# Sigmoids one by one behind later passes, weight passes behind them, and more filler matmuls between the first weight parts, in an mLSTM + two-MoE kernel

## The chip, the cores and the metric

One core of one Trainium2 chip runs the whole program in one launch. The metric is the time of an execution on the device in microseconds (us), lower is better. In the profile the engines are PE (matrix multiplies; PEld is its loading of the stationary operand), DVE (vector), ACT (scalar, activation functions), POOL (GpSimd) and SP, which issues the DMAs.

## What is computed

The reference is an mLSTM recurrence over 768 steps (2 batches, 8 heads of width 40), then two feed-forward layers over the 1536 tokens, each 320 to 2048 to 320 with an activation between.

```python
for t in range(S):                                   # per batch and head
    m_new = np.maximum(f_gate[t] + m, i_gate[t])
    f_stab, i_stab = np.exp(f_gate[t] + m - m_new), np.exp(i_gate[t] - m_new); m = m_new
    C = f_stab * C + i_stab * outer(v[t], k[t]);  n = f_stab * n + i_stab * k[t]
    o = 1.0 / (1.0 + np.exp(-o_gate[t]))
    y[t] = o * (C @ q[t]) / np.maximum(np.abs(n @ q[t]), 1.0)
h = x @ w_in;  x = (h - np.tanh(h)) @ w_out          # first layer
h = x @ w_in2; out = (h * np.tanh(softplus(h))) @ w_out2   # second layer
```

## The kernel before

**Tiles and stages.** The recurrence is computed in chunks of 128 steps (6 chunks, 2 batches: 12 jobs, `attention(j)`, lines 296 to 409), two jobs to a block of 256 tokens. A block's result, multiplied by the sigmoid of the o gates, is transposed (`transpose_x`, tile `xT`) and goes into the first layer. That layer runs in tiles of 256 tokens by two weight parts of 128 hidden columns, 16 parts in all: `mm1(i)` fills the PSUM tile `h` with 8 matmuls a part, `tile1(i)` makes the activation `g` of it and splits it into a rounded half `gh` (ACT) and a rest `gl` (POOL), and `mm2(i)` adds 12 matmuls a tile into `acc`, two tiles behind. Block 0 meets only the parts f = 0 to 7 first (tiles 0 to 3, `CUT[0] = 8`), while the weights still arrive.

**Weights.** They come as 64-bit floats and are turned into two rounded 32-bit halves in `conv_w` (lines 185 to 215). For each part f there are a shift on DVE (L196), a scaling pass on ACT (L204, `scaled`), a shift-and-or on DVE (L208, `third`), a rounding copy on ACT (L211, tile `w`, first half) and a subtraction on DVE (L213 and L214, second half). The first four matmuls of a part in `mm1` need L211, the next two L213 and the last two L214 as well.

**What sets the order.** Each engine runs its own instructions in one fixed order. A scheduler writes this order out when the program is built; `with after(x)` makes an instruction stand behind `x` on the same engine, and it adds no wait on the chip. So an instruction that has to wait holds everything behind it on its engine.

**Sigmoids.** `session(c0, c1, ...)` (line 681) issues one sigmoid over 128 x 640 for each chunk and, at its end, a small Exp that loads the other function table again. The sigmoid of chunk 0 runs near the start. Those of chunks 1 to 5 are given out in the loop over tiles, at i = 1, 2 and 3 (line 841), each with one instruction to stand behind. The first of them needs one table load, the Exp behind the last another.

**Fills.** `spin(n)` (line 633) issues n matmuls of 512 columns on constant data; nobody reads them. `keep(3, y)` in `mm1` (line 542) puts three of them behind each of the first six weight parts.

**Attention in between.** `ahead(n)` (line 770) moves the next attention jobs along by steps, so their matmuls (`nb`, `sc`, `it`, `pv`, `st`) stand among those of the tiles. `rest_t` (line 491) makes the decays `uT` and `dec`, once.

Of the kernel before, what the change touches and what calls it, by code (L numbers as in the profile page):

```python
# [11 lines left out]
AF = mybir.ActivationFunctionType  # L12
# [13 lines left out]
def kernel(  # L26
# [101 lines left out]

    texp, tbl, dls, tanhs = [], [], [], []

    scored, gated, rounded = {}, {}, {}

    spq, cvd, hold = [], [], []

# [50 lines left out]
    def conv_w(layer, f, first=(), behind=()):  # L185
        r = raw.pop((layer, f)).rearrange("p (n t) -> p n t", t=2)
        lo32, z = r[:, :, 0], r[:, :, 1]
        zf = z.bitcast(F32)
        w = wp.tile([P, WT], F32R, tag="w", name="w")
        wf = w.bitcast(F32)  # L190

        head = texp if (layer, f) == (0, 0) else tanhs if layer == 0 and f < CUT[0] else []
        with after(first):
            nc.vector.tensor_scalar(lo32, in0=lo32, scalar1=29, scalar2=None, op0=ALU.logical_shift_right)  # L196
        if second:
            nc.vector.scalar_tensor_tensor(
                lo32, in0=z, scalar=0x80000000, in1=lo32, op0=ALU.bitwise_and, op1=ALU.bitwise_or
            )  # L200
            scaled[layer, f] = nc.scalar.activation(out=zf, in_=zf, func=AF.Copy, scale=2.0 ** -111)
        else:
            with after(head):
                scaled[layer, f] = nc.scalar.activation(  # L204
                    out=zf, in_=zf, func=AF.Prelu, scale=2.0 ** -111, alpha=-2.0 ** 32
                )
        with after(behind):
            third[layer, f] = nc.vector.scalar_tensor_tensor(  # L208
                z, in0=z, scalar=3, in1=lo32, op0=ALU.logical_shift_left, op1=ALU.bitwise_or
            )  # L210
        cvd[:] = [nc.scalar.activation(out=w[:, 0:WC], in_=zf, func=AF.Copy)]  # L211
        eng = nc.gpsimd if (layer, f) == (0, 0) else nc.vector
        eng.tensor_tensor(w[:, WC:WT], in0=zf[:, 0:REM0], in1=wf[:, 0:REM0], op=ALU.subtract)  # L213
        lows[layer, f] = eng.tensor_tensor(w[64:P, REM0:REM1], in0=zf[64:P, REM0:REM1], in1=wf[64:P, REM0:REM1], op=ALU.subtract)  # L214
        wtile[layer, f] = w
# [203 lines left out]
    def gates():  # L419
        def row(name):  # L420
            return wp.tile([BH, S], F32, tag="w", name=name)

        i_t, f_t, F_t, g_t, u_t, rm = (row(n) for n in ("gi", "gf", "gF", "gg", "gu", "grm"))
        nc.sync.dma_start(out=f_t, in_=fg)
        nc.sync.dma_start(out=i_t, in_=ig)
        ch = lambda t: t.rearrange("p (c s) -> p c s", s=L)
        nc.vector.memset(n_all[:, 0:EC * L], 0.0)
        nc.vector.memset(rm, 1.0)
        nc.vector.memset(ch(rm)[:, :, 0:1], 0.0)
        nc.gpsimd.memset(na[0].bitcast(F32), 0.0)  # L430
        nc.gpsimd.memset(g_t, 0.0)
        nc.gpsimd.memset(ch(u_t)[:, 0:1, :], 0.0)
        nc.gpsimd.tensor_tensor(sel, in0=ident[:, 0:BH], in1=ident[:, 32:32 + BH], op=ALU.add)

        def scans(a, e):
            nc.vector.tensor_tensor_scan(
                out=F_t[:, a:e], data0=rm[:, a:e], data1=f_t[:, a:e], initial=0.0, op0=ALU.mult, op1=ALU.add
            )
            nc.vector.tensor_tensor(i_t[:, a:e], in0=i_t[:, a:e], in1=F_t[:, a:e], op=ALU.subtract)
            if not a:  # L440
                nc.vector.tensor_scalar(na[0][0:BH], in0=i_t[:, a:e], scalar1=-1.0, scalar2=None, op0=ALU.mult)
            if a:
                nc.vector.tensor_copy(ch(g_t)[:, 1:NCH, 0:1], ch(F_t)[:, 0:NCH - 1, L - 1:L])
            return nc.vector.tensor_tensor_scan(
                out=n_t[:, a:e], data0=g_t[:, a:e], data1=i_t[:, a:e], initial=n_t[:, a - 1:a] if a else -1e30,
                op0=ALU.add, op1=ALU.max,
            )

        def parts(k):
            cols = slice(k * L, (k + 1) * L)  # L450
            if k:
                nc.vector.tensor_scalar(na[k][0:BH], in0=i_t[:, cols], scalar1=-1.0, scalar2=None, op0=ALU.mult)
            nc.vector.tensor_copy(n0[k], n_all[:, cols])
            nc.vector.scalar_tensor_tensor(
                na[k][32:32 + BH], in0=i_t[:, cols], scalar=-1.0, in1=na[k][0:BH].bitcast(F32), op0=ALU.mult,
                op1=ALU.subtract,
            )
            return nc.vector.tensor_tensor(
                n0[k][32:64], in0=n_all[0:32, cols], in1=n0[k][0:32].bitcast(F32), op=ALU.subtract
            )  # L460

        scans(0, L)
        first = parts(0)

        def rest():
            with after([first]):
                scans(L, S)
            return rest_n

        def rest_n():  # L470
            for n, t in enumerate((n_t, i_t)):
                t, hi, lo = t[:, EC * L:S], nr[64 * n:64 * n + BH], nr[64 * n + 32:64 * n + 32 + BH]
                with after(texp):
                    copy_r(0, hi, t)
                with after([lows[0, 1]]):
                    nc.vector.tensor_tensor(lo, in0=t, in1=hi.bitcast(F32), op=ALU.subtract)
            return rest_u

        def rest_u():
            mp = once.tile([BH, NCH, 1], F32, name="mp")  # L480
            nc.vector.tensor_tensor(
                mp[:, 1:NCH, :], in0=ch(n_t)[:, 0:NCH - 1, L - 1:L], in1=ch(F_t)[:, 0:NCH - 1, L - 1:L], op=ALU.add
            )
            with after(dls):
                nc.gpsimd.tensor_tensor(
                    ch(u_t)[:, 1:NCH, :], in0=ch(n_t)[:, 1:NCH, :], in1=mp[:, 1:NCH, :].to_broadcast([BH, NCH - 1, L]),
                    op=ALU.subtract,
                )
            return rest_t

        def rest_t():
            with after(tbl):
                nc.scalar.activation(out=u_t, in_=u_t, func=AF.Exp, scale=-1.0)
            u_ps = at_ps([P, NCH, BH], "u_ps")
            for c in range(NCH):
                nc.tensor.transpose(u_ps[:, c, :], ch(u_t)[:, c, :], ident[0:BH, 0:BH])
            nc.vector.tensor_copy(uT, u_ps)

            ue = once.tile([BH, BH, NCH], F32, name="ue")
            nc.vector.tensor_tensor(  # L500
                ue, in0=ident[0:BH, 0:BH].rearrange("p (h o) -> p h o", o=1).to_broadcast([BH, BH, NCH]),
                in1=ch(u_t)[:, :, L - 1].rearrange("p (o c) -> p o c", o=1).to_broadcast([BH, BH, NCH]), op=ALU.mult,
            )
            d_ps = at_ps([P, B, HG, NCH], "d_ps")
            for r in range(2):
                nc.tensor.matmul(
                    d_ps[HP * r:HP * (r + 1)], lhsT=ones[0:BH, :],
                    rhs=ue.rearrange("p (b r g) c -> p r b g c", r=2, g=HG)[:, r], start=True, stop=True,
                )
            nc.vector.tensor_copy(dec, d_ps)  # L510

        return rest, first

# [11 lines left out]
    def mm1(i):  # L525
# [6 lines left out]
        for k, f in enumerate(fs):  # L532
# [6 lines left out]
                    )  # L539
            hold[:] = [y] if i < CUT[0] // NP - 1 else []  # L540
            if i < 3:
                keep(3, y)
        hps[i] = t

    def split_g(i, g, n):
# [5 lines left out]
    def tile1(i):  # L551
# [8 lines left out]
        nc.scalar.activation(out=u, in_=u, func=AF.Square, scale=G_SA)  # L560
        mark[:] = [nc.vector.tensor_tensor(g, in0=u, in1=h, op=ALU.mult)]  # L561
        nc.vector.tensor_tensor(t, in0=h, in1=t, op=ALU.subtract)  # L562
        nc.scalar.activation(out=u, in_=u, func=AF.Relu, bias=bias[:, 0:1])  # L563
        nc.vector.copy_predicated(out=g, mask=u.bitcast(U32), data=t)  # L564
        split_g(i, g, n)

# [13 lines left out]
    def mm2(i):  # L580
# [18 lines left out]
        if fs[-1] + 1 in ends_ or fs[-1] == NF - 1:  # L599
            more = l == 0 and fs[-1] + 1 > CUT[bi]  # L600
            for t, a in enumerate(accs.pop((l, bi))):
# [9 lines left out]
                for o, x in parts:  # L611
                    if more:
                        nc.vector.scalar_tensor_tensor(o, in0=x, scalar=sc, in1=o, op0=ALU.mult, op1=ALU.add)
                    elif l == 0 or t % 2:
                        nc.scalar.activation(out=o, in_=x, func=AF.Copy, scale=sc)  # L615
                    else:
                        nc.vector.tensor_scalar(o, in0=x, scalar1=sc, scalar2=None, op0=ALU.mult)
                if l:
# [10 lines left out]
    def program():  # L629
# [50 lines left out]

        def session(c0, c1, end=True, behind=()):
            for n, c in enumerate(range(c0, c1)):
                with after(texp + [x for x in behind[n:n + 1]]):
                    sig.append(sigmoid_o(B * c, B))
            if end:
                with after(sig):
# [107 lines left out]
        def conv_to(i, bi, f):  # L794
            if i < n_s:
                lead1(min(CUT[0], f + PRE + NP), start)
            elif i < n_0:
                lead1(
                    CUT[0] + -(-(NF - CUT[0]) * min(i - n_s + CY, n_0 - n_s) // (n_0 - n_s)), mark + [gated[max(gated)]]
                )  # L800
            elif conv1[0] == NF:
                lead2(min((i - n_0 + 2) // R2, E2))
# [5 lines left out]
        for i in range(len(tiles)):  # L808
# [28 lines left out]
            mm1(i)  # L837
            if l == 0:
                tile1(i)
                if 0 < i < 4:  # L840
                    session(2 * i - 1 - (i > 1), 2 * i, i == 3, [rounded[i - 2] if i > 2 else scaled[0, 7], rounded[i - 1]] if i > 1 else [rounded[0]])
                qm.append(i)
                if len(qm) > LAG:
                    mm2(qm.pop(0))
                if i:
                    ahead(min(int(14 * (k + (i - i0 + 1) / n_seg + 0.4)), 14 * NB if i > 2 else 14))
                if k >= T2:
                    next(sg, None)
                    next(sg, None)
# [72 lines left out]
```

## Time and profile before

| What | Value |
|---|---|
| Time, median of 3 runs | 461.39 us (461.31 to 461.73) |
| Time of the profiled execution | 462.71 us |
| Its span from the first to the last instruction | 460.9 us, mean granted clock 0.981 |
| PE busy | 446.3 us, 97% of the span |
| DVE, ACT, POOL busy | 299.7, 283.5, 105.1 us |

PE is busy nearly all the time, so what can change the total is where PE waits, how fast its clock runs, and how much work it is given. The profiled execution is 1.3 us above the median; 1.8 us of its time lie outside the span. A change of the program is read as a difference and set against the median.

### The profile page before, as it was taken

The page shows a single profiled execution, that of the slowest core. Times are in us where ns is not written, and L with a number is a line of the kernel's source. Part 1 is how long each engine was busy: PE and PEld are TensorE (multiplying, and loading weights), DVE is VectorE, ACT ScalarE, POOL GpSimd, SP SyncE. Part 2 cuts the span into 40 slices and gives each one's busy share as a digit, 9 for nine tenths or more (in the row PEclk, how much of TensorE's full clock was granted, in tenths as well). Part 3 has the DMA queues.
Part 4 walks back from the last instruction along what each step waited for, and adds up shares of the span by engine and source line. Part 5 has one row for each costly group of instructions (what it writes and reads, how often), then busy time and mean ns, then how long its engine had stood idle before and what let it go on. Part 6 is the DMA issues. An engine that isn't in the chain of part 4 may idle for free. (4 is left out here: it accounts for less than half of the span.)

```text
span 460.9 us, 7944 instructions
## 1 busy us (share of the span) xinstructions
PE 446.3 (97%) x3092; PEld 405.9 (88%) x3092; DVE 299.7 (65%) x526; ACT 283.5 (62%) x517; POOL 105.1 (23%) x119
## 2 busy tenths in 40 slices
PE   9878999999999999999999999999999999999997
PEld 5645978979999999999999998999889899988996
DVE  7898398977978878558879987989822211221112
ACT  7678657777575865799797877756633333332231
POOL 2304215644275232243332332000000000000000
PEclk9979599999999999999999999999999999999999
DMA  8984444631333301001111120244000000010001
GB/s 255 377 287 130 159 117 129 185 94 48 105 130 95 118 9 57 1 0 65 64 33 56 55 82 30 78 173 154 37 28 30 1 0 1 1 58 0 1 0 57
DMA packets 22728, 38.03 MB, mean 83 GB/s; under 512 B 1348, under 2 KB 17028, under 8 KB 22692
## 3 DMA queue, kind: packets, MB, share of 16 engines
q1 hardware_dynamic: 22692, 37.54, 25.0%
q8 instruction: 24, 0.39, 0.4%
q14 instruction: 12, 0.10, 0.1%
HBM read 35.41 MB, written 1.97 MB: 81 GB/s over the span
## 5 line engine op out<-in xcount | busy, mean ns | idle before, releaser
L536 PE MATMUL h<-xT,w 128*128 128x256 f32 (+1 forms) x1152 | 210.8, 325 | 5.0 <-ACT w L211 2.2
L536 PEld LDWEIGHTS h<-xT,w 128*128 128x128 f32 x1152 | 171.1, 191 | 22.3 <-ACT w L211 2.3
L596 PE MATMUL acc<-w,gh 128*128 128x320 f32 x384 | 120.0, 314 | 3.0 <-ACT gh L547 2.5
L597 PE MATMUL acc<-w,gh 128*128 128x320 f32 x384 | 119.7, 313 | 0.0
L598 PE MATMUL acc<-w,gl 128*128 128x320 f32 x384 | 115.4, 313 | 0.1
L548 POOL TENSOR_TENSOR gl<-g,gh 128x512 fp32r<-128x512 f32 x48 | 64.7, 1349 | 121.5 <-ACT gh L547 114.8
L577 DVE TENSOR_TENSOR gl<-g,gh 128x512 fp32r<-128x512 f32 x48 | 33.1, 691 | 88.5 <-ACT g L576 88.4
L596 PEld LDWEIGHTS acc<-w,gh 128*128 128x128 f32 x384 | 72.5, 189 | 6.1 <-ACT gh L547 3.0
L575 ACT ACTIVATE gh<-h 128x512 fp32r<-128x512 f32 x48 | 28.7, 598 | 75.7 <-PE h L536 75.6
L597 PEld LDWEIGHTS acc<-w,gh 128*128 128x128 f32 x384 | 72.5, 189 | 2.9 <-issue 0.4
L598 PEld LDWEIGHTS acc<-w,gl 128*128 128x128 f32 x384 | 70.7, 189 | 1.0 <-POOL gl L548 0.3
L564 DVE COPY_PREDICATED g<-u,t 128x512 f32<-128x512 uint32 x48 | 39.9, 833 | 12.3 <-ACT u L563 12.0
L561 DVE TENSOR_TENSOR g<-u,h 128x512 f32<-128x512 f32 x48 | 32.7, 682 | 23.3 <-ACT u L560 15.7
L547 ACT ACTIVATE gh<-g 128x512 fp32r<-128x512 f32 x48 | 30.3, 632 | 16.8 <-DVE g L564 12.4
L563 ACT ACTIVATE u<-u,bias 128x512 f32<-128x512 f32 x48 | 34.8, 726 | 7.9 <-DVE g L561 7.8
L558 ACT ACTIVATE u<-h 128x512 f32<-128x512 f32 x48 | 28.3, 590 | 13.1 <-PE h L536 12.8
L211 ACT ACTIVATE w<-raw 128x704 fp32r<-128x704 f32 x32 | 27.3, 863 | 13.7 <-DVE raw L208 13.5
L562 DVE TENSOR_TENSOR t<-h,t 128x512 f32<-128x512 f32 x48 | 32.9, 684 | 0.0
L213 DVE TENSOR_TENSOR w<-raw,w 128x576 fp32r<-128x576 f32 x31 | 26.9, 867 | 6.4 <-ACT w L211 6.3
L560 ACT ACTIVATE u<-u 128x512 f32<-128x512 f32 x48 | 30.5, 636 | 0.0
L208 DVE SCALAR_TENSOR_TENSOR raw<-raw 128x704 uint32<-128x704 uint32 x32 | 29.0, 917 | 0.4
L576 ACT ACTIVATE g<-h 128x512 f32<-128x512 f32 x48 | 28.6, 595 | 0.0
(104 smaller groups left out, 451.9 us busy)
## 6 DMA issues: line engine op xcount, KB each, us to landing
raw<-in_w_dram SPq DMA_DIRECT2D x32, 704.0 KB
qk_t<-in_qk_dram SPq DMA_DIRECT2D x12, 512.0 KB
kv_t<-in_kv_dram SPq DMA_DIRECT2D x12, 324.0 KB
out_dram<-xo SPq DMA_DIRECT2D x12, 160.0 KB
xo<-in_og_dram SPq DMA_DIRECT2D x2, 800.0 KB
xo<-in_og_dram SPq DMA_DIRECT2D x1, 320.0 KB
sd<-nr SPq DMA_DIRECT2D x20, 4.0 KB
md<-nr SPq DMA_DIRECT2D x10, 8.0 KB
```

The costliest lines, as they stand in the source:

```text
L536: y = nc.tensor.matmul(t[:, k * nt:(k + 1) * nt], lhsT=w[:, o:o + P], rhs=x[:, kk, :], start=(n == 0), stop=(n == len(pairs) - 1),)
L547: rounded[i] = nc.scalar.activation(out=gh, in_=g, func=AF.Copy)
L548: nc.gpsimd.tensor_tensor(gl, in0=g, in1=gh.bitcast(F32), op=ALU.subtract)
L560: nc.scalar.activation(out=u, in_=u, func=AF.Square, scale=G_SA)
L561: mark[:] = [nc.vector.tensor_tensor(g, in0=u, in1=h, op=ALU.mult)]
L562: nc.vector.tensor_tensor(t, in0=h, in1=t, op=ALU.subtract)
L563: nc.scalar.activation(out=u, in_=u, func=AF.Relu, bias=bias[:, 0:1])
L564: nc.vector.copy_predicated(out=g, mask=u.bitcast(U32), data=t)
L577: mark.append(nc.vector.tensor_tensor(gl, in0=g, in1=gh.bitcast(F32), op=ALU.subtract))
L596: turn(lambda: nc.tensor.matmul(a, lhsT=gh[:, sl], rhs=wh, start=(f in ends_), stop=False))
L597: turn(lambda: nc.tensor.matmul(a, lhsT=gh[:, sl], rhs=wl, start=False, stop=False))
L598: turn(lambda: nc.tensor.matmul(a, lhsT=gl[:, sl], rhs=wh, start=False, stop=end))
```

## The change

The sigmoids of chunks 1 and 2 are given out at tile 2 and those of chunks 3 to 5 at tile 3, each behind a later instruction: the newest L211 copy, the Relu of tile 2, the rounding of tile 2, the Relu of tile 3 and the rounding of tile 3. The fills behind the first six weight parts become 3, 8, 5, 5, 2, 2 instead of 3 each. The two copies of `uT` and `dec` out of PSUM move from DVE to ACT. In the first eight parts a scaling pass stands behind that of the part before. The conversion of the first parts after tile 3 stands behind the rounding of tile 3. The first copies of `acc` into `xo` stand behind the newest copy of `xT`, and `ahead` may take 8 steps instead of 14 at tile 1.

```diff
         head = texp if (layer, f) == (0, 0) else tanhs if layer == 0 and f < CUT[0] else []
+        if layer == 0 and f:
+            head = head + [scaled[0, f - 1]]
...
-            nc.vector.tensor_copy(uT, u_ps)
+            copy_r(0, uT, u_ps)
...
-            nc.vector.tensor_copy(dec, d_ps)
+            copy_r(0, dec, d_ps)
...
             if i < 3:
-                keep(3, y)
+                keep((3, 8, 5, 5, 2, 2)[f], y)
...
-        nc.scalar.activation(out=u, in_=u, func=AF.Relu, bias=bias[:, 0:1])
+        relus[i] = nc.scalar.activation(out=u, in_=u, func=AF.Relu, bias=bias[:, 0:1])
...
-                        nc.scalar.activation(out=o, in_=x, func=AF.Copy, scale=sc)
+                        with after(chain[1:2] if l == bi == 0 else []):
+                            nc.scalar.activation(out=o, in_=x, func=AF.Copy, scale=sc)
...
-                with after(texp + [x for x in behind[n:n + 1]]):
+                with after(texp + sig[-1:] + list(behind[n:n + 1])):
...
-                    CUT[0] + -(-(NF - CUT[0]) * min(i - n_s + CY, n_0 - n_s) // (n_0 - n_s)), mark + [gated[max(gated)]]
+                    CUT[0] + -(-(NF - CUT[0]) * min(i - n_s + CY, n_0 - n_s) // (n_0 - n_s)), mark + [gated[max(gated)]] + [rounded[i - 1]] * (i == n_s)
...
-                if 0 < i < 4:
-                    session(2 * i - 1 - (i > 1), 2 * i, i == 3, [rounded[i - 2] if i > 2 else scaled[0, 7], rounded[i - 1]] if i > 1 else [rounded[0]])
+                if 1 < i < 4:
+                    session(2 * i - 3, 2 * i - 1 + (i > 2), i == 3, [cvd[0], relus[2]] if i < 3 else [rounded[2], relus[3], rounded[3]])
...
-                    ahead(min(int(14 * (k + (i - i0 + 1) / n_seg + 0.4)), 14 * NB if i > 2 else 14))
+                    ahead(min(int(14 * (k + (i - i0 + 1) / n_seg + 0.4)), (8, 14)[i - 1] if i < 3 else 14 * NB))
```

On ACT, from the tanhs of tile 2 to the rounding of its result: `u`, `t`, `gh` are tiles of the activation, `raw` and `w` those of the weights, `Dm` one of the attention, `xo` that of the sigmoids. Line numbers of the changed kernel are 2 or 3 higher. Before:

```order
44 L558 ACTIVATE u<-h 128x512
45 L559 ACTIVATE t<-h 128x512
46 L204 ACTIVATE raw<-raw 128x704
47 L560 ACTIVATE u<-u 128x512
48 L338 ACTIVATE Dm<-nb 128x512
49 L257 ACT_TABLE_LOAD
50 L257 ACTIVATE xo<-xo 128x2x320 x2
51 L547 ACTIVATE gh<-g 128x512
52 L257 ACTIVATE xo<-xo 128x2x320 x2
53 L204 ACTIVATE raw<-raw 128x704
54 L211 ACTIVATE w<-raw 128x704 x2
55 L563 ACTIVATE u<-u,bias 128x512
```

And in the changed kernel:

```order
49 L562 ACTIVATE u<-u 128x512
50 L213 ACTIVATE w<-raw 128x704
51 L549 ACTIVATE gh<-g 128x512
52 L340 ACTIVATE Dm<-nb 128x512
53 L213 ACTIVATE w<-raw 128x704
54 L259 ACT_TABLE_LOAD
55 L259 ACTIVATE xo<-xo 128x2x320
56 L565 ACTIVATE u<-u,bias 128x512
57 L259 ACTIVATE xo<-xo 128x2x320
58 L549 ACTIVATE gh<-g 128x512
59 L259 ACTIVATE xo<-xo 128x2x320
60 L560 ACTIVATE u<-h 128x512
```

The rounding `gh` of tile 1 and the two copies `w` of parts 6 and 7 now stand ahead of the table load and of all five sigmoids; before, two and four sigmoids stood ahead of them. The number of table loads is the same.

On PE, the matmuls of part 1 and what follows, up to those of part 2 (`w_ps` is written by a fill, `u_ps` and `d_ps` by the decays). Before:

```order
67 L536 MATMUL h<-xT,w 128x256 x4
68 L636 LDWEIGHTS const-bfloat16-1.0
69 L636 MATMUL w_ps<-const-bfloat16-1.0 32x512
...
74 L506 MATMUL d_ps<-ue,ones 64x48 x2
75 L536 MATMUL h<-xT,w 128x256 x8
```

And in the changed kernel:

```order
67 L538 MATMUL h<-xT,w 128x256 x4
68 L639 LDWEIGHTS const-bfloat16-1.0
69 L639 MATMUL w_ps<-const-bfloat16-1.0 32x512
...
84 L508 MATMUL d_ps<-ue,ones 64x48 x2
85 L538 MATMUL h<-xT,w 128x256 x8
```

Eight fills instead of three (two rows each) now stand between the matmuls of part 1 and those of part 2.

On DVE, the end of the first attention pair behind block 0 and the second halves of its `xT`, in the changed kernel:

```order
93 L198 TENSOR_SCALAR raw<-raw 128x704 x2
94 L411 TENSOR_TENSOR C_99<-C_99,st 40x4x41 x2
95 L210 SCALAR_TENSOR_TENSOR raw<-raw 128x704 x2
96 L286 TENSOR_TENSOR xT<-xt,xT 128x3x128 x2
97 L215 TENSOR_TENSOR w<-raw,w 128x576
```

And before:

```order
92 L196 TENSOR_SCALAR raw<-raw 128x704 x2
93 L284 TENSOR_TENSOR xT<-xt,xT 128x3x128
94 L409 TENSOR_TENSOR C_99<-C_99,st 40x4x41 x2
95 L564 COPY_PREDICATED g<-u,t 128x512
96 L208 SCALAR_TENSOR_TENSOR raw<-raw 128x704 x2
97 L284 TENSOR_TENSOR xT<-xt,xT 128x3x128
```

Both subtractions of `xT` now stand behind both passes L208 (now L210); before, one of them stood ahead.

## Rows read from the trace of the kernel before

**Rows 1.** PE by stretch: window, its length, busy (matmuls), granted clock, DMA share, GB/s.

```profile
29.00:35.70 6.70, 6.14 (x19) 0.50 0.72 240
46.00:56.20 10.20, 9.66 (x47) 0.50 0.41 136
65.70:100.00 34.30, 32.59 (x270) 1.00 0.41 126
100.00:461.00 361.00, 356.49 (x2427) 1.00 0.16 52
```

**Rows 2.** Timeline of PE: start us, length, engine, line, operation, idle before and its releaser.

```profile
24.59 0.82 PE L636 MATMUL w_ps<-const-bfloat16-1.0 128*32 128x512 bf16 x3
...
27.86 0.74 PE L536 MATMUL h<-xT,w 128*128 128x256 f32 x4 [2.19 <-ACT w L211]
29.56 1.23 PE L536 MATMUL h<-xT,w 128*128 128x256 f32 x4 [0.96 <-DVE w L213]
30.71 1.46 PE L636 MATMUL w_ps<-const-bfloat16-1.0 128*32 128x512 bf16 x3
...
46.53 0.63 PE L596 MATMUL acc<-w,gh 128*128 128x320 f32 x1 [2.49 <-ACT gh L547]
```

**Rows 3.** Timeline of ACT from the tanhs of tile 2 to the rounding of tile 2.

```profile
40.45 0.60 ACT L558 ACTIVATE u<-h 128x512 f32<-128x512 f32 x1 [1.18 <-PE h L536]
40.95 0.59 ACT L559 ACTIVATE t<-h 128x512 f32<-128x512 f32 x1
41.43 0.87 ACT L204 ACTIVATE raw<-raw 128x704 f32<-128x704 f32 x1
42.17 0.63 ACT L560 ACTIVATE u<-u 128x512 f32<-128x512 f32 x1
42.69 0.60 ACT L338 ACTIVATE Dm<-nb 128x512 f32<-128x512 f32 x1
43.31 1.28 ACT L257 ACT_TABLE_LOAD   x1
44.60 1.36 ACT L257 ACTIVATE xo<-xo 128x640 f32<-128x640 f32 x2
45.87 0.61 ACT L547 ACTIVATE gh<-g 128x512 fp32r<-128x512 f32 x1
46.39 1.35 ACT L257 ACTIVATE xo<-xo 128x640 f32<-128x640 f32 x2
47.64 0.82 ACT L204 ACTIVATE raw<-raw 128x704 f32<-128x704 f32 x1
48.37 1.56 ACT L211 ACTIVATE w<-raw 128x704 fp32r<-128x704 f32 x2
49.83 0.71 ACT L563 ACTIVATE u<-u,bias 128x512 f32<-128x512 f32 x1
52.22 0.63 ACT L547 ACTIVATE gh<-g 128x512 fp32r<-128x512 f32 x1 [1.68 <-DVE g L564]
```

**Rows 4.** Timeline of DVE: a decay copy, the step ahead of gh of tile 1, two waits.

```profile
26.48 0.24 DVE L497 COPY uT<-u_ps 128x96 f32<-128x96 f32 x1
...
40.74 0.74 DVE L564 COPY_PREDICATED g<-u,t 128x512 f32<-128x512 uint32 x1
...
49.22 0.76 DVE L213 TENSOR_TENSOR w<-raw,w 128x576 fp32r<-128x576 f32 x1 [3.62 <-ACT w L211]
...
57.78 0.50 DVE L382 TENSOR_TENSOR hv<-hv,pv 128x328 f32<-128x328 f32 x1 [4.03 <-PE pv L378]
```

**Rows 5.** Timeline of PE at the first tile of block 1.

```profile
65.73 0.97 PE L536 MATMUL h<-xT,w 128*128 128x256 f32 x6 [0.58 <-ACT xT L283]
...
67.68 0.98 PE L335 MATMUL nb<-md,sd 128*128 128x512 f32 x2 [0.51 <-ACT Dm L338]
...
69.80 0.37 PE L356 MATMUL sc<-qk_t 64*128 64x128 f32 x1 [0.26 <-DVE xT L284]
```

**Rows 6.** The page, part 5: the pass L208, with busy time and mean ns.

```profile
L208 DVE SCALAR_TENSOR_TENSOR raw<-raw 128x704 uint32<-128x704 uint32 x32 | 29.0, 917 | 0.4
```

More of the change, by code (lines that the diff above doesn't have):

```diff
@@ L129 @@
     texp, tbl, dls, tanhs = [], [], [], []
-    scored, gated, rounded = {}, {}, {}
+    scored, gated, rounded, relus = {}, {}, {}, {}
     spq, cvd, hold = [], [], []
```

## Prediction

> **What bounds the kernel now.** I read the page's parts 1 and 2 first: PE is busy for 97% of the span, and the row of granted clock is low in a few slices near the start and nowhere else. A table of windows then splits PE [rows 1]. From 100 us on PE is busy for 356.49 of 361.00 us at full clock, and from 65.7 to 100 us for 32.59 of 34.30. The reader is to see that no edit can give much there: the matmuls are the bound, and this change leaves their number as it is. Two stretches differ. From 29.0 to 35.7 and from 46.0 to 56.2 us the granted clock is 0.50, which is 1.2 instead of 2.4 GHz, and PE is busy for 6.14 and 9.66 us. Had the same matmuls run at full clock, they would have taken half: 3.07 and 4.83 us are lost there.
>
> The timeline of PE shows what goes ahead of each [rows 2]. Ahead of the first, PE ends three fills and the decays' small matmuls at about 25.7 us, waits 2.19 us for the copy `w` (L211) of part 2, does four matmuls and waits 0.96 us for L213. Ahead of the second it waits 2.49 us, until 46.53, for `gh` of tile 1. Together that is 5.64 us of idling and 7.90 us of slow clock in the first 57 us.
>
> Why `gh` is late stands in the timeline of ACT [rows 3]. Its input was complete at 41.48 (40.74 plus 0.74) [rows 4], but on ACT a scaling pass, a Square, a `Dm`, the table load (1.28 us) and two sigmoids stand ahead of it, so it starts at 45.87. Behind it two more sigmoids hold the copies `w` of parts 6 and 7 until 48.37, and these hold the Relu of tile 2 (49.83), and so its rounding, until 52.22. That is one ACT queue in which work that nobody needs soon, the sigmoids, stands ahead of work that PE waits for.
>
> **The change part by part.** I make the sum as differences within the profiled execution of 462.71 us, which is 1.32 above the median of 461.39, and set it against that median.
>
> (a) Sigmoids behind, weight copies ahead. Take ACT's step from start to start from [rows 3]: 0.5 for a tanh, Square or `gh`, 0.73 for a pass over 704 columns, 0.62 for `Dm`, 1.29 for the table load, 0.64 for a sigmoid. In the new order the tanhs of tile 2 can start at 39.27 (40.45 less the 1.18 that it waited for PE), plus 0.25 from (c): 39.5. Then come the second tanh, scaling, Square, the copy of part 6 (41.7 to 42.6), `gh` of tile 1 (42.5 to 43.1), `Dm`, the copy of part 7 (43.6 to 44.4), the table load and a sigmoid to 46.3, the Relu (0.71), a sigmoid and `gh` of tile 2 at 47.7. So `gh` of tile 1 comes 3.4 us earlier, the copies 4.8 to 6.7 us and `gh` of tile 2 4.5 us. If the first low stretch goes too, PE arrives at this place at 44.04 - 3.07 - 0.8 + 1.5 (terms c, d and e) = 41.7. It then waits about 0.9 us for part 6 and 0.3 for its second half: 1.2 instead of 2.49, **-1.3**.
>
> (b) The second low stretch. PE then has no idle time over about 1 us between 37 and 57 us, where the stretches that kept full clock had similar waits: 0.58, 0.51 and 0.26 us within five us at 65 to 70 [rows 5]. So I take its loss as gone, **-4.8**. Bounds: 0 and -4.83.
>
> (c) Eight fills behind part 1. Five more at 0.213 us (512 columns at 2.4 GHz; three take 0.82 with the tail of the last [rows 2]) cover 1.07 us of the 2.19. The copy of `uT` goes on ACT ahead of the tanhs and so of L211 of part 2. No row has it on ACT. It lies between DVE's 0.24 [rows 4] and the 0.60 of a `Dm` four times as wide [rows 3]; at 96 columns it is nearer the first, so 0.25. That of `dec` delays only the copy of part 3, for which PE doesn't wait. The waits become 2.19 - 1.07 + 0.25 = 1.37, and 0.96 as before, since DVE waits for ACT's Square and so moves by the same 0.25: **-0.8**. What DVE saves is swallowed by that wait.
>
> (d) The first low stretch. Ahead of its fall PE waited 3.15 us, with one group of four matmuls (0.74 us) between the waits [rows 2]. With the fills it waits 2.33. At 65 to 70 us it waited 1.35 in all and the clock stayed full [rows 1, 5]. The new case lies between these two, so this is the least sure term: **-3.07** if the clock stays full, 0 if not. I take the first: the fills take the longest wait apart.
>
> (e) Fills. 25 instead of 18, seven more, all in PE's one queue: 7 x 0.213 = **+1.5** at full clock (+3.0 at half the clock, as three at 30.71 us take 1.46 [rows 2]). I count them in full, because the waits are counted by themselves.
>
> (f) The edge to block 1. Both subtractions of `xT` now stand behind two passes L208 of 0.92 us [rows 6], and ACT makes the scaling of three parts ahead of the `xT` copies. Before, PE waited 1.35 us there [rows 5]. Bounds: nothing more, or two passes, 1.83. The passes start earlier as well, so I take **+0.75**.
>
> (g) Order and hand-overs. From 65.7 to 100 us PE idled 1.71 of 34.3 us, 0.05 a us [rows 1]. For some 25 us of new order I add that rate, **+1.2**. The scaling order, the four `acc` copies ahead of `Dm` and the other limit of `ahead` I cost at nothing: the matmuls of tiles 4 and 5, which PE has ready there, cover them. Uncovered, the copies, each half as wide as a `Dm` of 0.60 us or less [rows 3], would be some 1.3 us. DMAs: the raw weights of parts 8 to 10 are issued when L214 of parts 5 to 7 has freed a buffer, which gets earlier, so SP's queue gains slack.
>
> Sum: -1.3 - 4.8 - 0.8 - 3.07 + 1.5 + 0.75 + 1.2 = -6.5. The profiled execution would be 456.2, the median **454.9 us**.
>
> One rule bears on (a). The row says that the table load takes 1.28 us and that the first sigmoid starts 1.29 us after it [rows 3].
>
> The Trainium skill ("ScalarE: Activation LUTs", What ACT_TABLE_LOAD costs) puts each switch at about 2.66 us, with a drain of 1.38 beside the load, and advises to do all functions of a table set before switching, which speaks against sigmoids strewn between other functions. By that price the Relu and the rounding of tile 2 would come 1.4 us later, and the sum, as an estimate from that page, would be -5.1 at worst. The trace shows no such drain, so I stay with the row.
>
> **The rivals.**
>
> B. Only the second low stretch goes. If 2.33 us of waiting is still too much, the clock falls at 29 us as before, ten fills instead of six run in the slow stretch (+0.85), and PE arrives so late that the 2.49 us wait vanishes whole: -4.8 - 2.5 - 0.8 + 1.5 + 0.85 + 0.75 + 1.2 = -3.8, 457.6 us. For it: two waits of 1.37 and 0.96 us remain. Against it: they stand apart, and PE works more between them.
>
> C. The first goes, but another low stretch comes in the 40s, because PE now waits for part 6 at 42 us. As long as the first it gives 3.07 back (457.9), as long as the second 4.83 (459.7): about 458.8 us. Against it: PE has the matmuls of parts 4 and 5 right ahead.
>
> D. Every wait that is removed comes back at the edge to block 1, where DVE and ACT must first make `xT`: 461.4 us, no change. Against it: DVE idled 3.62 us for the late copies `w` and 4.03 us for `pv` [rows 4], so it has room to be earlier.
>
> E. Slower: the slow clock stays. The seven fills are then pure load in a slow queue. With both low stretches as before the sum is -1.3 - 0.8 + 3.0 + 0.75 + 1.2 = +2.85, 464.2 us. The terms other than the clock add up to +1.35, so this decides once the low clock covers more than about 15.8 - 2.7 = 13.1 us of PE's busy time. For it: a low stretch of 10 us shows that the clock does not come back at once. Against it: the wait that went ahead of the second stretch is halved.
>
> **How the numbers follow.** Chances: forecast 0.48, B 0.22, C 0.14, D 0.06, E 0.10. The predicted time is that of the first, 454.9, whose own range is 453 to 456.5 (terms f and g at their ends). 452.5 to 460.3 takes in A to C and leaves out D and E and something below: about 0.2. A difference of 0.2%, 0.9 us, is about what a measurement of this kernel tells from none. Faster: the first three and a little of D, 0.86; within: most of D, 0.05; slower: 0.09.
>
> **What the profile after would show.** Granted clock 1.00 from 29 to 57 us (B: low to about 36; C: low in the 40s; E: both). PE's wait for `gh` of tile 1 gone and one under 1 us for L211 of part 6 in its place. The wait ahead of part 2 near 1.4 us. `gh` of tile 1 at 42 to 43 us and that of tile 2 near 48. The first matmul of tile 4 at about 60 instead of 65.73. It would be wrong if ACT, with the weight copies moved up, hands tile 2's Relu to DVE late enough that PE runs dry before tile 3, or if the fills themselves hold matmuls that were ready.

## Result and profile after

The changed kernel takes **458.35 us** (median of 5 runs, 457.39 to 458.68), the kernel before 461.73 beside it (461.31 to 463.34): a ratio of 0.9916 with an interval of 0.9894 to 0.9939. It is faster, by 3.4 us instead of the 6.5 predicted. Two more series of the same program against before gave 0.9881 and 0.9893 (below).

The profiled execution took 457.39 us (span 455.4, clock 0.993), against 462.71 (460.9, 0.981). The page after, engines and granted clock:

```profile
PE 444.0 (97%) x3099; PEld 403.0 (88%) x3099; DVE 299.9 (66%) x524; ACT 284.2 (62%) x519; POOL 105.1 (23%) x119
...
PEclk9799999999999999999999999999999999999999
```

PE by stretch after (window, length, busy, granted clock, DMA share, GB/s), the first four lines as in [rows 1] and one from nearer the start:

```profile
29.00:35.70 6.70, 5.24 (x27) 1.00 0.82 250
...
46.00:56.20 10.20, 9.78 (x86) 1.00 0.64 196
...
66.00:100.00 34.00, 33.37 (x282) 1.00 0.46 139
100.00:461.00 361.00, 350.43 (x2387) 1.00 0.16 50
...
16.00:23.50 7.50, 7.50 (x59) 0.54 1.09 346
```

Both stretches that had 0.50 run at 1.00; from 46.0 to 56.2 us PE does 86 matmuls instead of 47 in about the same busy time. But a low stretch now lies from 16 to 23.5 us, in code that the change leaves alone and that ran at full clock in the profile before.

PE after, in order of time, against [rows 2] and [rows 5]:

```profile
26.30 1.91 PE L639 MATMUL w_ps<-const-bfloat16-1.0 128*32 128x512 bf16 x8
...
29.50 0.74 PE L538 MATMUL h<-xT,w 128*128 128x256 f32 x4 [1.03 <-ACT w L213]
31.20 0.82 PE L538 MATMUL h<-xT,w 128*128 128x256 f32 x4 [0.96 <-DVE w L215]
...
43.77 0.74 PE L538 MATMUL h<-xT,w 128*128 128x256 f32 x4 [0.92 <-ACT w L213]
...
46.42 0.50 PE L538 MATMUL h<-xT,w 128*128 128x256 f32 x2 [0.86 <-DVE w L215]
...
62.47 0.97 PE L538 MATMUL h<-xT,w 128*128 128x256 f32 x6
64.23 0.96 PE L337 MATMUL nb<-md,sd 128*128 128x512 f32 x3 [0.79 <-DVE xT L286]
```

Because of the early low stretch PE comes to the fills behind part 1 at 26.30 instead of 24.59 us, yet it starts tile 4 at 62.47 instead of 65.73, with 416 matmuls done by then instead of 396 (seven of the 20 are fills). The wait for `gh` of tile 1 is gone; two short ones for the weights of part 6 stand there instead.

ACT after, against [rows 3]:

```profile
42.87 0.85 ACT L213 ACTIVATE w<-raw 128x704 fp32r<-128x704 f32 x1
43.62 0.61 ACT L549 ACTIVATE gh<-g 128x512 fp32r<-128x512 f32 x1
...
44.62 0.84 ACT L213 ACTIVATE w<-raw 128x704 fp32r<-128x704 f32 x1
45.47 1.28 ACT L259 ACT_TABLE_LOAD   x1
46.77 0.74 ACT L259 ACTIVATE xo<-xo 128x640 f32<-128x640 f32 x1
47.41 0.71 ACT L565 ACTIVATE u<-u,bias 128x512 f32<-128x512 f32 x1
...
50.11 0.63 ACT L549 ACTIVATE gh<-g 128x512 fp32r<-128x512 f32 x1 [1.36 <-DVE g L566]
```

`gh` of tile 1 starts at 43.62 (before 45.87), that of tile 2 at 50.11 (before 52.22), although ACT's chain began later. The latter waits for DVE in both (1.68 and 1.36 us); what moved is the Relu ahead of it, from 49.83 to 47.41. PE is busy 2.3 us less (446.3 to 444.0) and idle 3.2 us less (span less busy, 14.6 to 11.4).

### The profile page after: what moved, and what is told of

Same layout as the page of the kernel before. It is cut to its first block, busy times and chain, and to the rows that moved or that the text cites. A ratio compares the mean times of both kernels' runs of the same rounds, so it can differ in the third digit from the quotient of the medians.

```text
span 455.4 us, 7958 instructions
## 1 busy us (share of the span) xinstructions
PE 444.0 (97%) x3099; PEld 403.0 (88%) x3099; DVE 299.9 (66%) x524; ACT 284.2 (62%) x519; POOL 105.1 (23%) x119
## 5 line engine op out<-in xcount | busy, mean ns | idle before, releaser
L538 PE MATMUL h<-xT,w 128*128 128x256 f32 (+1 forms) x1152 | 205.9, 321 | 4.9 <-ACT w L213 1.9
L538 PEld LDWEIGHTS h<-xT,w 128*128 128x128 f32 x1152 | 167.9, 189 | 21.9 <-ACT w L213 2.3
L562 ACT ACTIVATE u<-u 128x512 f32<-128x512 f32 x48 | 30.5, 639 | 0.0
L210 DVE SCALAR_TENSOR_TENSOR raw<-raw 128x704 uint32<-128x704 uint32 x32 | 29.1, 921 | 0.5
L561 ACT ACTIVATE t<-h 128x512 f32<-128x512 f32 x48 | 28.8, 599 | 0.0
(104 smaller groups left out, 452.5 us busy)
```

The costliest lines, as they stand in the source:

```text
L538: y = nc.tensor.matmul(t[:, k * nt:(k + 1) * nt], lhsT=w[:, o:o + P], rhs=x[:, kk, :], start=(n == 0), stop=(n == len(pairs) - 1),)
```

## The experiments

Kernels of one series ran on one chip beside the same runs of the kernel before. The low clock is told as stretches of the profiled execution, and for all executions of a kernel as the mean granted clock.

**First series: the change again, and three variants of it** (before: median 463.53, 11 runs).

The changed kernel once more:

> The changed kernel once more, for a second profile. Theory 1 (the shortfall against the forecast is a low-clock stretch whose place is not fixed by the program; in the first profile it lay at 16.7 to 23.6 us, in code that the change left alone): 457.4 to 458.7 us, and the low stretch lies elsewhere, has another length, or is absent. Rival (the change itself makes the clock fall there): the low stretch at 16 to 24 us again.

It took 457.34 us (457.11 to 460.18), ratio 0.9881 (0.9851 to 0.9910). Windows of its PE, and its waits ahead of part 2:

```profile
20.50:24.50 4.00, 4.00 (x16) 0.57 1.01 316
31.00:35.00 4.00, 4.00 (x16) 0.57 0.99 315
```

```profile
28.79 0.74 PE L538 MATMUL h<-xT,w 128*128 128x256 f32 x4 [1.03 <-ACT w L213]
30.49 0.89 PE L538 MATMUL h<-xT,w 128*128 128x256 f32 x4 [0.96 <-DVE w L215]
```

The same program has its low clock at other places. Its waits of 1.03 and 0.96 us are those of the first profile; there the clock stayed full behind them, here it fell.

Six more fills near the start:

```diff
-        keep(4, chain[0])
+        keep(10, chain[0])
```

> The changed kernel with ten fills instead of four behind the first transpose, where PE waits about 1.5 us in the kernel before. Theory 1 (the early fall comes from this wait): no low stretch ahead of 24 us, PE's work there unchanged since the fills stand in the wait, 456.5 to 457.5 us. Rival (the early fall does not matter or has another cause): 458.0 to 459.6, the upper end if the six fills hold matmuls that were ready (6 x 0.21 us).

It took 457.39 us (455.88 to 459.25), 0.9873 (0.9841 to 0.9906). The first line is those fills, the second a window of PE:

```profile
16.33 2.35 PE L639 MATMUL w_ps<-const-bfloat16-1.0 128*32 128x512 bf16 x10
```

```profile
44.50:48.50 4.00, 3.84 (x16) 0.57 0.63 191
```

This profile has full clock from 16 to 23.5 us, but so has one of the three of the changed kernel. In six executions the mean granted clock is 0.996 against 0.9925 of the kernel above. Yet the times can't be told apart. At full clock six fills are 6 x 0.213 = 1.3 us of work.

The old fills in the changed kernel:

```diff
-                keep((3, 8, 5, 5, 2, 2)[f], y)
+                keep(3, y)
```

> The changed kernel with three fills behind each part as before. Theory 1 (the fills keep the clock up ahead of part 2): a low stretch from about 29 us comes back, 2 to 4 us slower than the changed kernel, 460 to 462 us. Rival (fills are only load, the order on ACT made the gain): 457 to 458 us.

It took 456.63 us (455.98 to 459.73), 0.9860 (0.9829 to 0.9891): not told apart from the changed kernel. PE waits 2.32 us ahead of part 2 again, and a low stretch follows from 30.5 to 34 us (0.53). The theory that needs the eight fills put this at 460 to 462: the low stretch came, the time did not, and the theory falls.

The old sigmoids in the changed kernel:

```diff
-                with after(texp + sig[-1:] + list(behind[n:n + 1])):
+                with after(texp + [x for x in behind[n:n + 1]]):
...
-                if 1 < i < 4:
-                    session(2 * i - 3, 2 * i - 1 + (i > 2), i == 3, ...)
+                if 0 < i < 4:
+                    session(2 * i - 1 - (i > 1), 2 * i, i == 3, ...)
```

> The changed kernel with the sigmoids given out as before (tiles 1, 2 and 3); the scheduler then sets the rounding of tile 1 ahead of the table load, but four sigmoids ahead of the copy of part 7 and the Relu of tile 2. Theory 1: part 7, the Relu and the rounding of tile 2 come 2 to 3 us later, PE waits for them, 1 to 2.5 us slower than the changed kernel, 459.5 to 461 us. Rival (only the fills matter): 458.3 us.

It took 458.84 us (458.07 to 462.14), 0.9911 (0.9878 to 0.9944): 1.5 us more than the changed kernel in this series, with intervals that overlap, and just below the 459.5 of theory 1. ACT shows that the sigmoids did not go back to their old place:

```profile
43.51 0.62 ACT L549 ACTIVATE gh<-g 128x512 fp32r<-128x512 f32 x1
...
44.64 1.28 ACT L259 ACT_TABLE_LOAD   x1
45.94 2.62 ACT L259 ACTIVATE xo<-xo 128x640 f32<-128x640 f32 x4
48.46 0.83 ACT L213 ACTIVATE w<-raw 128x704 fp32r<-128x704 f32 x1
```

With the rest of the change in place, the scheduler puts `gh` of tile 1 ahead of the table load by itself; only the copy of part 7 and the Relu of tile 2 stand behind four sigmoids. So this run undoes half of the new order, and most of the gain stays; what the other half is worth it doesn't tell from nothing.

**Second series: parts of the change put into the kernel before** (before: median 463.28, 29 runs).

The kernel before, unchanged:

> The kernel before once more, for a second profile. Theory 2 (the place of a low-clock stretch differs from execution to execution; the order on ACT behind tile 1 made the gain): low stretches that begin elsewhere than at 28.9 and 46.0 us, and a time anywhere from 461 to 465.5 us. Rival (the falls are tied to PE's waits): low from 29 and from 46 us again.

It took 462.76 us (461.71 to 464.93, 12 runs), 1.0000 (0.9982 to 1.0018). Windows of its PE, and its first wait of part 2:

```profile
16.00:23.50 7.50, 7.50 (x60) 0.54 1.10 350
...
29.50:37.00 7.50, 6.67 (x23) 0.54 0.68 220
46.50:57.50 11.00, 9.64 (x48) 0.53 0.40 123
```

```profile
29.43 0.87 PE L536 MATMUL h<-xT,w 128*128 128x256 f32 x4 [2.13 <-ACT w L211]
```

Here the kernel before has the early stretch too, beside those of [rows 1]. So that stretch is not an effect of the change. The other two came again behind the same waits, as the rival had it (2.13 us ahead of part 2, 2.50 for `gh` of tile 1).

The new fills alone:

```diff
-                keep(3, y)
+                keep((3, 8, 5, 5, 2, 2)[f], y)
```

> The kernel before with 3, 8, 5, 5, 2, 2 fills alone. The scheduler then sets the rounding of tile 1 and the copy of part 6 ahead of the table load by itself, and leaves part 7 and the Relu of tile 2 behind four sigmoids. Theory 2: close to the run with the old sigmoids, 458 to 460.5 us. Rival (fills are only load and the order that they bring about does not matter): 461.5 to 465 us.

It took 461.44 us (460.61 to 463.12, 12 runs), 0.9959 (0.9941 to 0.9977): 1.8 us less, between theory 2 (up to 460.5) and its rival (from 461.5). ACT, and PE's longest wait after 40 us:

```profile
41.66 0.66 ACT L547 ACTIVATE gh<-g 128x512 fp32r<-128x512 f32 x1
...
42.82 1.28 ACT L257 ACT_TABLE_LOAD   x1
44.12 2.62 ACT L257 ACTIVATE xo<-xo 128x640 f32<-128x640 f32 x4
...
47.37 0.82 ACT L211 ACTIVATE w<-raw 128x704 fp32r<-128x704 f32 x1
```

```profile
61.66 0.42 PE L596 MATMUL acc<-w,gh 128*128 128x320 f32 x1 [2.21 <-ACT gh L547]
```

The edit touches PE alone, yet the scheduler now writes the rounding of tile 1 ahead of the table load. So this run doesn't tell the fills apart from the order on ACT. The wait for that rounding is gone, and one of 2.21 us for the `gh` of a later tile stands near the edge to block 1.

The new sigmoids alone, each also behind the one before, with the limit of `ahead` that they need:

```diff
-                if 0 < i < 4:
-                    session(2 * i - 1 - (i > 1), 2 * i, i == 3, [rounded[i - 2] if i > 2 else scaled[0, 7], rounded[i - 1]] if i > 1 else [rounded[0]])
+                if 1 < i < 4:
+                    session(2 * i - 3, 2 * i - 1 + (i > 2), i == 3, [cvd[0], relus[2]] if i < 3 else [rounded[2], relus[3], rounded[3]])
```

> The kernel before with the sigmoids given out as in the change alone (with the limit of ahead that this needs). The order on ACT has the rounding of tile 1 and the copies of parts 6 and 7 ahead of the table load. Theory 2: all of the gain or nearly, 456.5 to 458.5 us. Rival (fills or the later conversion are needed too): 459.5 us or more.

It took 458.68 us (457.33 to 460.03), 0.9908 (0.9889 to 0.9927): 4.6 us less, just above the 458.5 of theory 2 and below the rival's 459.5. No wait of PE after 40 us is longer than 1.27 us, and tile 4 starts at 62.37.

Only `gh` of tile 1 ahead of the table load:

```diff
-                    session(2 * i - 1 - (i > 1), 2 * i, i == 3, [rounded[i - 2] if i > 2 else scaled[0, 7], rounded[i - 1]] if i > 1 else [rounded[0]])
+                    session(2 * i - 1 - (i > 1), 2 * i, i == 3, [rounded[i - 2] if i > 2 else scaled[0, 7], rounded[i - 1]] if i > 1 else [rounded[1]])
```

with each sigmoid also behind the one before.

> The kernel before with the first sigmoid behind the rounding of tile 1 and each sigmoid behind the one before: on ACT only the rounding of tile 1 changes places with the table load and two sigmoids; four sigmoids still stand ahead of parts 6 and 7. Theory 2a (PE's wait for that rounding is the largest term): the wait of 2.5 us goes, one of about 1.2 us for part 6 comes, 459.5 to 462 us. Rival 2b (the copies of parts 6 and 7 are what counts): as the kernel before, within 1 us.

It took 460.58 us (457.94 to 462.80, 12 runs), 0.9935 (0.9911 to 0.9958): 2.7 us less. ACT, and PE's longest wait after 40 us:

```profile
44.60 0.64 ACT L560 ACTIVATE u<-u 128x512 f32<-128x512 f32 x1
...
45.60 0.64 ACT L547 ACTIVATE gh<-g 128x512 fp32r<-128x512 f32 x1
46.26 1.28 ACT L257 ACT_TABLE_LOAD   x1
47.55 2.62 ACT L257 ACTIVATE xo<-xo 128x640 f32<-128x640 f32 x4
50.08 0.82 ACT L204 ACTIVATE raw<-raw 128x704 f32<-128x704 f32 x1
50.79 1.56 ACT L211 ACTIVATE w<-raw 128x704 fp32r<-128x704 f32 x2
```

```profile
65.00 0.66 PE L281 MATMUL xt<-ident,xo 128*128 128x128 f32 x2 [2.47 <-issue]
```

This execution ran late, with low clock from 13.5 to 24 us (0.51) and from 31 to 37.5 (0.50), so starts are read against the Square ahead (`u<-u`): `gh` begins 1.0 us after it, before 3.7 [rows 3]. One rounding of 0.64 us that stands ahead of the table load and two sigmoids, not behind them, gives more than half of what the new place of all five gives, by the medians; the two intervals overlap. The long low stretch behind the wait for `gh` is gone too (46.0 to 56.2 us: 1.00). The copies of parts 6 and 7 still stand behind four sigmoids, and a wait of 2.47 us is left at the edge to block 1, as one of 2.21 was with the fills alone. In the kernels with the new sigmoids no wait there is over 1.44 us.

**Third series: what the fills and the conversion are worth** (before: median 462.86, 11 runs).

No fills behind the weight parts at all (`keep(0, y)` in the changed kernel):

> The changed kernel with no fill behind any weight part (25 fewer). Theory 3 (fills are load that PE pays for where nothing waits, and they keep the clock up only now and then): no slower than with old fills, 455 to 457.5 us; 18 fills less than that run are 3.8 us of load, half of which stands in waits. Rival (fills hold the clock up): low stretches over 10 us in the profile and 459 us or more.

It took 459.91 us (458.67 to 460.90), 0.9931 (0.9908 to 0.9954). The theory that the fills are mere load, with 455 to 457.5, falls: without them it is 2.2 us slower than with them in this series. The rival (low stretches over 10 us in all, 459 us or more) came out. Two windows of PE, and its waits:

```profile
25.50:32.50 7.00, 4.09 (x18) 0.51 0.74 250
42.50:49.50 7.00, 6.13 (x32) 0.52 0.19 67
```

```profile
28.07 1.22 PE L538 MATMUL h<-xT,w 128*128 128x256 f32 x4 [2.53 <-ACT w L213]
...
43.37 2.07 PE L358 MATMUL sc<-qk_t 64*128 64x128 f32 x14 [2.38 <-DVE Dm L362]
```

The 25 fills are 25 x 0.213 = 5.3 us of work, but without them PE idles 18.5 us in its profile instead of 11.8 (span less busy). The fills stand mostly in time that PE had to wait anyway. The order on ACT changes with them too, so this is not the effect of the fills alone.

Only the first two groups (3 and 8, then none):

```diff
-                keep((3, 8, 5, 5, 2, 2)[f], y)
+                keep((3, 8, 0, 0, 0, 0)[f], y)
```

> The changed kernel with 3 and 8 fills behind parts 0 and 1 and none behind parts 2 to 5. Theory 3: 455.5 to 457.5 us. Rival (the fills behind parts 2 to 5 hold the clock up): a low stretch from the 30s on and 459 us or more.

It took 459.30 us (458.16 to 460.13), 0.9917 (0.9896 to 0.9938), 1.6 us above the changed kernel (the intervals overlap), with a low stretch from 15.5 to 23 and another at 73.5 to 77.5 us. Theory 3 falls here too; of the rival the time came, and the low stretch from the 30s on did not.

The new sigmoids alone, and the conversion after tile 3 behind the rounding of tile 3:

```diff
-                    CUT[0] + -(-(NF - CUT[0]) * min(i - n_s + CY, n_0 - n_s) // (n_0 - n_s)), mark + [gated[max(gated)]]
+                    CUT[0] + -(-(NF - CUT[0]) * min(i - n_s + CY, n_0 - n_s) // (n_0 - n_s)), mark + [gated[max(gated)]] + [rounded[i - 1]] * (i == n_s)
```

> The kernel before with the new sigmoids, and the conversion of the parts after tile 3 put behind the rounding of tile 3 as in the change; fills, copies and scaling order as before. Theory 4 (this clause makes up what the sigmoids alone lack against the changed kernel with old fills): 456.3 to 457.5 us. Rival: as the sigmoids alone, 458.7 us.

It took 459.10 us (458.02 to 460.26), 0.9918 (0.9897 to 0.9939). The theory that this edit makes up what the sigmoids alone lack, with 456.3 to 457.5, falls.

The changed kernel, last in the series:

> The changed kernel a third time, beside the runs above. Theory 1: 457 to 458.7 us, one or two low stretches at places that differ again from 16.7 to 23.5 and from 20.6 to 24.2 and 31.1 to 34.5 us. Rival: at one of those places again.

It took 457.73 us (457.11 to 459.12), 0.9893 (0.9869 to 0.9916). Windows of its PE, where it has the first low stretch of [rows 1]:

```profile
16.00:23.50 7.50, 6.08 (x64) 1.00 1.09 350
28.50:36.00 7.50, 6.53 (x21) 0.54 0.71 222
```

The low stretch overlaps the second one of the second profile (31 to 35) and lies behind the waits of part 2 (1.09 and 0.97 us), as in the kernel before.

## Why the prediction was right in direction and too large in size

**The mechanism was right.** Seven kernels with the sigmoids in the new place (the changed one, with early fills, old fills, two groups of fills, no fills, sigmoids alone, sigmoids with the conversion) stand at 0.986 to 0.993. The rounding of tile 1 alone gives 0.9935, the fills alone 0.9959, and these too moved that rounding. So the order on ACT carries most of the gain, as the sigmoids alone (with their limit of `ahead`) show; what the fills do without it was not isolated. What sets the kernel with the sigmoids alone (0.9908) apart from the whole change (0.9893) is not to be told from nothing; with the conversion too they stand 1.4 us above it in one series, with intervals that overlap. The scaling order, the decay copies and the copies of `acc` were not tried one by one.

**The step that failed is the clock: terms (b) and (d), -7.9 us together.** Between the two profiled executions PE's busy time, which holds the clock and the fills, was to fall by 6.4 us (b, d, e) and fell by 2.3; its idle time was to fall by 0.15 (a, c, f, g) and fell by 3.2. The price of the clock was wrong in two ways.

First, I took both low stretches for removed with the longest waits, and put any other at nothing. For (b) that held: in all three profiles of the changed kernel the long one behind the wait for `gh` of tile 1 is gone, which both profiles of the kernel before have. For (d) it held in the first profile alone. In the two others a low stretch still follows the waits of part 2 (31 to 35 and 28.5 to 36 us), and two of the three have one ahead of 25 us (16 to 23.5, 20.5 to 24.5) that the sum didn't have. The change lowered how much there is, not to nothing:

| | executions | mean time, us | mean granted clock | span x (1 - clock), us |
|---|---|---|---|---|
| before, all series but the first pair | 63 | 463.30 | 0.982 | 8.5 |
| changed, first pair and two series | 17 | 458.00 | 0.993 | 3.4 |

So 5.1 us of low clock went by this rough measure, which counts half of each low stretch, its idle time too; by it the one profile of before has 460.9 x 0.019 = 8.8, where the 7.9 is half of the busy time alone. (For the first pair's runs of the kernel before no clock is on record.)

Second, I counted each us of it as a us of time. Over 146 executions of all kernels, each compared with the mean of its own kernel in its own series, a us more of this lost clock goes with 0.42 us more span (standard error 0.04). Single executions scatter about it: one of the changed kernel with a mean clock of 1.00 took 457.33 us, like two at 0.992 (457.17 and 457.35), and one of the kernel with early fills at 1.00 took 455.88, the least of its six. The two profiles of the kernel before show a reason. The second has the stretch from 16 to 23.5 us besides, worth 7.5 x 0.46 = 3.4 us of the rough measure. The first has full clock there and this wait, which the second doesn't have:

```profile
19.33 0.62 PE L281 MATMUL xt<-ident,xo 128*128 128x128 f32 x3 [1.48 <-DVE xo L392]
```

So the second reaches part 2 at 29.43 instead of 27.86, 1.6 us later and not 3.4, and its span is 1.9 us longer (462.8 and 460.9): a late PE waits less. The three profiles of the changed kernel can't show this: each has about as much low clock (0.992 or 0.993), and they start tile 4 at 62.47, 62.21 and 62.46. The rate comes from executions that differ by themselves, not from an edit; if it holds across kernels, the clock made some 0.42 x 5.1 = 2.1 of the 5.3 us between the means above, and waits and order the rest, 3.2.

**The other terms** were to add up to +1.35, and so were too dear by several us, which hid part of the first error. From the profile:

- (a) -1.3: 2.49 us of waiting for `gh` became 0.92 + 0.86 = 1.78 in the first profile, a gain of 0.7; in the two others only 0.72 stays, a gain of 1.8. Right in place and about right in size. `gh` of tile 1 came at 43.62, within a us or so of the 42.5 forecast, but that of tile 2 at 50.11 instead of 47.7: 1.36 us of that is its wait for DVE, and the rest ACT's later chain. (Part 7's copy began at 49.10 before, the second of the two in the merged row, so its forecast gain was 5.5 us and not 4.8; no term rests on it.) Tile 4 was forecast at about 60 and came at 62.47.
- (c) -0.8: the wait ahead of part 2 fell from 2.19 to 1.03 us (forecast 1.37), and 0.96 stayed. The `uT` copy on ACT took 0.25 us, as bounded.
- (e) +1.5: not isolated. With 18 fills instead of 25 the time is the same or a little less; with none it is 2.2 us more. Fills cost little where they stand in a wait.
- (f) +0.75: wrong in sign. At the edge PE waited 1.35 us before and 0.32 + 0.79 = 1.11 after: DVE's two passes added nothing there.
- (g) +1.2: an allowance that the profile does not bear out. From 66 to 100 us PE idles 0.63 us of 34.0, where it idled 1.71 of 34.3 before.

**The rivals.** D (all given back at the edge) and E (slower) did not happen. The first pair's 458.35 lies between B (457.6) and C (458.8), but not by their mechanism: the low clock of that profile lies at neither place. The last profile is nearly B as described: the second stretch gone, the first as before, and its series has 457.73 us against 457.6. That the times agree is luck: the gain of that series is 5.1 us and not B's 3.8, and PE still waits 0.72 us at part 6. The wide range, 452.5 to 460.3, holds 458.35 because it takes in B and C; the forecast's own, 453 to 456.5, doesn't.

The first pair's gain of 3.4 us and the 6.2 and 5.1 us of the later medians come from both sides: the changed kernel's medians are 458.35, 457.34 and 457.73, those of before 461.73, 463.53 and 462.86. The kernel before moved more, 1.8 us against 1.0; why its first runs were the fastest of them is open. The step from profile to median also cost: the profile before lay 1.32 us above its median, that of the changed kernel 0.96 below its own, which makes 2.3 of the 3.4 us by which 454.9 missed. Between the profiles the sum missed by 1.2 us (456.2 against 457.39).

No version tried is shown to be faster than the changed kernel; the one with the old fills (0.9860) overlaps with it.

## What to carry to other kernels

On an engine with one fixed order, look for work that nobody needs soon ahead of a short instruction that another engine waits for: moving one rounding of 0.64 us ahead of a table load and two sigmoids went with 2.7 us (1.9 to 4.1). Don't price a low-clock stretch of one profile at half its busy time: ask whether it lies at the same place in a second profile, and whether PE waits behind it anyway. Don't carry a profile's distance from the median over to another kernel. Filler matmuls inside a wait cost nothing that these runs could tell (18, 25 or 31 of them), so count them only as far as they reach beyond it.

## What the runs showed that was not expected

The same program, on the same data, has its low-clock stretches at different places from one execution to the next, and once in 17 executions of the changed kernel a mean clock of 1.00. The same waits (1.03 and 0.96 us) were followed by full clock in one profile and by 0.57 in another.

The table load costs its 1.28 us and no more in the new place either: the sigmoid behind it starts at 46.77, 1.30 us after the load. The Trainium skill ("ScalarE: Activation LUTs", What ACT_TABLE_LOAD costs) adds a drain of 1.38 us to each switch; no run here shows one, and the estimate of -5.1 made from it is not borne out by that wait, however near the -5.3 between the two profiled executions. Both kernels have five table loads, so a price per switch doesn't tell them apart.
